# A state-space convolution mixed with a gated feed-forward: rewritten with two equal passes, turned tables and one written order

## The chip, the cores and the metric

The kernel runs on one core of a Trainium2 chip. A core has five instruction streams that run side by side and wait for one another through semaphores: PE (TensorE, matrix products), DVE (VectorE, elementwise), ACT (ScalarE, elementwise with function tables), POOL (GpSimd) and SP (SyncE), which here issues every transfer. Operands lie in SBUF (128 partitions), matrix products land in PSUM (eight banks of 512 float32 values a partition), and inputs, output and spilled intermediates lie in DRAM. The metric is device time in microseconds (us); less is better.

## The reference

The inputs are a sequence of 2048 rows of 640 channels, the parameters of a diagonal state-space model with 128 complex states a channel, and the weights of a gated feed-forward.

```python
g = sigmoid((x * gate_w).sum(-1, keepdims=True))
a = A(x);  b = (gelu(x @ w_gate) * (x @ w_up)) @ w_down       # 640 -> 1728 -> 640
return g * a + (1 - g) * b

def A(u):
    dt = exp(log_dt)[:, None]
    P = exp((dt * (A_re + 1j*A_im))[:, :, None] * arange(L))     # (640, 128, 2048)
    K = einsum("dn,dnl,dn->dl", C, P, dt * B).real               # (640, 2048)
    y = irfft(rfft(pad(u)) * rfft(pad(K)))[:L]                   # a causal convolution of length 2048
    return y + u * Dskip
```

So there are four large pieces of work: the table K from sums of decaying oscillations over 128 states, the convolution of u with K, the two products that widen x to 1728 columns, and the product that narrows them again.

## The kernel before, in words

**K's tables.** A lag is written as l = a + b, with 21 values of a (`A_OF`) and 32 values of b (`b_of`, a multiple of 8). ACT makes the decays exp(a32 * a) and exp(a32 * b) into `eA` and `eB` (`exps`, lines 208 and 211). DVE makes the phases as integers, 65536 to a turn (`trig`, lines 236, 239, 243), ACT their sines and cosines (line 252), and DVE multiplies decays by them (`ktable`, lines 353 to 370). Positive and negative b share a sine up to its sign, so line 367 negates a table. PE contracts over the 128 states (`contract`, lines 382 and 384: 84 columns a product), and `gather` sorts the result with selection matrices (line 405) into `KTt`. This goes by parts of 128 channels, five in all.

**The convolution.** Blocks of 512 rows, c = 0 to 3, are folded (`u_fold`: sum and difference with the rows in reverse, which PE makes with a flip matrix, line 478; the result goes through DRAM as `PMd`), transformed (`u_forward`, line 574), and multiplied with the transformed blocks of K (`k_forward`, line 593, whose evictions are lines 556 and 559) by `products` (lines 631, 635, 636: three planes of K, the third a negated copy made at line 616). `inverse` transforms back (line 647), unfolds and adds u * Dskip (lines 655, 657), and ACT scales with g (line 660). The transform matrices are eleven tables `DFT` (`dft_matrix`).

**The feed-forward.** `ffn_up` makes gate and up for 256 columns of weights at a time (line 428: five products of 512 columns each, into a single bank), ACT or DVE evicts (lines 438 and 440), and SP stores to `GUd` in DRAM (line 441). `down` loads them again, ACT applies gelu (line 694), DVE multiplies (line 695), the result is also spilled to `HTd`, PE contracts over 1728 (line 706), ACT scales by 1 - g (line 708), DVE adds the other half and SP stores the output (`blend`, lines 668 and 669).

**Passes and order.** The second half of the kernel runs in two passes over channels, of 384 and 256 (`PASS`, `DS`): the first makes and spills the gelu product, the second reloads it. The program is written as loops; each engine gets its instructions in an order that a scheduler fixes at build time from the program's order and its own costs, and buffers come from pools that go round. In the first half the list `act` and `some_ups` mix table work with gate/up work; in the second the string of steps F, S, P, I, D, B does it. SP first loads six parameter arrays and u by transposing transfers (lines 133 and 489), then the weights (line 424).

Of the kernel before, what the change touches and what calls it, by code (L numbers as in the profile page):

```python
# [9 lines left out]
ALU = mybir.AluOpType  # L10
# [7 lines left out]
QUARTER = 16384.0  # L18
SIN_SCALE = 2.0 * math.pi / TURN * (1.0 - 2e-7)

A_OF = [0, 1, 2, 3, 4, 5, 6, 7, 256, 258, 260, 262, 512, 516, 768, 772, 1280, 1024, 1536, 1792, 2048]
NA = len(A_OF)
NB_ = 32
NQ = 5


MID = 128
NK = 17  # L30


def b_of(slot):
    return 16 + slot if slot < 16 else 31 - slot
# [3 lines left out]
def kernel(  # L38
# [18 lines left out]
    nc = tc.nc  # L57
    Bsz, L, D = A_u.shape
    N = A_A_re.shape[1]
    F = B_w_gate.shape[1]  # L60
    assert (Bsz, L, D, N) == (1, 2048, 640, 128)
    KT_ = D // 128
    NFT = (F + 127) // 128
    DP = 128
    NP = D // DP
    GP = DP // 4

    PASS = ((0, 1, 2), (3, 4))
    DS = [(DP * p[0], DP * (p[-1] + 1)) for p in PASS]
    DHM = DP * 3  # L70
    DO = D // 2
    NM = 4
# [3 lines left out]

    u_v = u2.rearrange("(c a p e) d -> p c a (e d)", c=4, a=2, p=128, e=2)
    out_v = out2.rearrange("(c a p e) d -> p c a (e d)", c=4, a=2, p=128, e=2)

    last_table = [None]  # L80

    def table(inst):

        if last_table[0] is not None:
            tc.add_manual_dep(inst.ins, last_table[0],
                              mybir.DependencyInfo(mybir.DependencyClass.NoSync, mybir.DependencyReason.DATA),
                              reason="table order")
        last_table[0] = inst.ins.name
        return inst

    def low16(ap):
        return ap.bitcast(I16)

    cp = ctx.enter_context(tc.tile_pool(name="konst", bufs=1))
    dp = ctx.enter_context(tc.tile_pool(name="spill", bufs=1, space=bass.MemoryType.DRAM))
    psC = ctx.enter_context(tc.tile_pool(name="psc", bufs=2, space=bass.MemoryType.PSUM))
    psF = ctx.enter_context(tc.tile_pool(name="psf", bufs=4, space=bass.MemoryType.PSUM))


    NMAT = 11  # L100
    M_E = 10
    DFT = cp.tile([128, NMAT, 2, 512], BF16, name="DFT")
    sel = cp.tile([128, 4, NB_], BF16, name="sel")
    diag = cp.tile([128, KT_, 128], BF16, name="diag")
    ident = cp.tile([128, 128], BF16, name="ident")
    flip = cp.tile([128, 128], BF16, name="flip")
    flipn = cp.tile([128, 128], BF16, name="flipn")
    gwc = cp.tile([128, KT_], BF16, name="gwc")
    KTt = cp.tile([128, NQ, D], BF16, name="KTt")
    T5 = cp.tile([128, D], BF16, name="T5")  # L110
    xT = cp.tile([128, KT_, 2, L // 2], BF16, name="xT")
    g32 = cp.tile([128, 16], FP32, name="g32")
    omg = cp.tile([128, 16], FP32, name="omg")
    rsd = dp.tile([1, 512], FP32, name="rsd")
    HTd = [dp.tile([128, 2, NFT, 256], BF16, name=f"HTd{c}") for c in range(4)]
    PMd = [dp.tile([128, 2, 2, D], BF16, name=f"PMd{c}") for c in range(4)]
    GUd = [[dp.tile([128, NFT, 2, 256], BF16, name=f"GUd{r}_{c}") for c in range(4)] for r in range(2)]

    kctx = ExitStack()
    pp = kctx.enter_context(tc.tile_pool(name="kparams", bufs=1))  # L120
    kb = kctx.enter_context(tc.tile_pool(name="ktab", bufs=1))

    eA = kb.tile([N, 3, NA, DP], BF16, name="eA")
    eB = kb.tile([N, 3, GP, NB_, 4], BF16, name="eB")
    fwk = kctx.enter_context(tc.tile_pool(name="fwork", bufs=2))
    pd = kctx.enter_context(tc.tile_pool(name="dftp", bufs=1))
    kw = kctx.enter_context(tc.tile_pool(name="kwork", bufs=1))
    ictx = ExitStack()
    pw = ictx.enter_context(tc.tile_pool(name="prep", bufs=1))

    def loadT(ap, name):
        t = pw.tile([N, D], BF16, name=name)
        nc.sync.dma_start_transpose(out=t[:], in_=ap[:, :])  # L133
        return t

    ldt = pw.tile([N, D], BF16, name="ldt")
    nc.sync.dma_start(out=ldt[:], in_=A_log_dt.partition_broadcast(N))
    AreT = loadT(A_A_re, "AreT")
    AimT = loadT(A_A_im, "AimT")
    CreT = loadT(A_C_re, "CreT")  # L140
    CimT = loadT(A_C_im, "CimT")
    BreT = loadT(A_B_re, "BreT")
    BimT = loadT(A_B_im, "BimT")
    dskc = pw.tile([128, KT_], BF16, name="dskc")
    nc.sync.dma_start(out=dskc[:], in_=A_Dskip.rearrange("(k p) -> p k", p=128))
    nc.sync.dma_start(out=gwc[:], in_=gate_w.rearrange("(k p) -> p k", p=128))

    xv_i = pw.tile([128, NK], I32, name="xv_i")
    nc.gpsimd.iota(xv_i[:], pattern=[[8, NK]], base=0, channel_multiplier=0)
    xv = pp.tile([128, NK], FP32, name="xv")  # L150
    nc.vector.tensor_copy(out=xv[:], in_=xv_i[:])

# [21 lines left out]
    for q, vals in ((0, (3, 1, 3, 1)), (1, (5, 3, 5, 3))):  # L174
        for g in range(4):
            nc.vector.memset(ncol[32 * g:32 * g + 32, q:q + 1], float(vals[g]))
# [195 lines left out]
    GB = 6  # L372
# [392 lines left out]
```

## Time and profile before

| | |
|---|---|
| time, median of 3 runs | 396.59 us (395.36 to 398.38) |
| span of the profiled execution | 393.3 us; its own time isn't given, 3.3 us lie between this span and the median |
| PE, DVE, ACT busy | 316.4, 302.1, 282.1 us |
| POOL busy | 5.0 us |
| bytes moved by transfers | 68.46 MB |
| granted PE clock, mean | 0.950 |

The span runs from the first to the last instruction. Busy time of an engine is the union of its instructions; a matrix product or an elementwise instruction overlaps the next one by its tail, so two durations in a row add up to more than the time they take. "Idle before" and the list of waits say for how long an engine stood still and what ended that. A window is a stretch of the span, with each engine's busy time in it.

### The profile page before, as it was taken

Reading aid. Unit: us, or ns where it says so; the run is one execution under the profiler, and the core shown is the slowest. Engines: PE = TensorE matmul, PEld = TensorE weight load, DVE = VectorE, ACT = ScalarE, POOL = GpSimd, SP = SyncE. Lnnn points to the kernel's source line nnn. Section 1 sums busy time; section 2 is a strip of 40 time slices with the busy share of each in tenths; the row PEclk is TensorE's granted clock in tenths of the full one; section 3 lists DMA queues with packets and bytes.
Section 4 is the critical chain, followed back from the end, with each engine's and each line's share of the span. In section 5 each row is a group of like instructions: output and inputs, shape, how many; then the busy total and the mean of one; then the engine's idle time right before and its main releaser. Section 6 shows DMA issues by size and latency. Waiting matters only on the chain.

```text
span 393.3 us, 6099 instructions
## 1 busy us (share of the span) xinstructions
PE 316.4 (80%) x2152; PEld 171.5 (44%) x2152; DVE 302.1 (77%) x555; ACT 282.1 (72%) x476; POOL 5.0 (1%) x39
## 2 busy tenths in 40 slices
PE   0019938599999998998379869989998987989994
PEld 0004413235446444544165325535545543557773
DVE  3994999869994989979920399879989798799500
ACT  6955999399986997896866996567669438434333
POOL 5000000000000000000000000000000000000000
PEclk9999987979999999999889977998999998999998
DMA  5893722374664477277449821587980688856760
GB/s 116 155 216 99 213 68 67 105 244 118 184 179 135 133 229 249 85 234 237 163 131 303 230 92 33 128 274 203 286 235 1 182 254 257 270 179 211 226 211 28
DMA packets 96815, 68.46 MB, mean 174 GB/s; under 512 B 22928, under 2 KB 92560, under 8 KB 96784
## 3 DMA queue, kind: packets, MB, share of 16 engines
q1 hardware_dynamic: 96784, 68.07, 60.0%
q8 instruction: 17, 0.28, 0.3%
q14 instruction: 14, 0.11, 0.1%
HBM read 37.96 MB, written 26.48 MB: 164 GB/s over the span
## 4 chain that ended last, share of the span: by engine, by line
PE 50%; ACT 22%; DMA 12%; SPq 6%; DVE 5%; issue 3%; ACTq 0%; DVEq 0%
PE gu L428 17%; PE gu L706 15%; PE cv L593 4%; ACT eA L208 4%; SPq L489 3%; DMA ph<-in_A_u_dram 3%; ACT eB L211 2%; ACT T L252 2%; PE cv L647 2%; ACT HT L694 2%; DMA pm<-PMd 2%; PE cv L405 2%; SPq L133 2%; PE cv L574 2%; PE gu L593 2%
## 5 line engine op out<-in xcount | busy, mean ns | idle before, releaser
L428 PE MATMUL gu<-xT,Wg 128*128 128x512 bf16 (+1 forms) x280 | 73.9, 394 | 39.0 <-DMA Wg<-in_B_w_gate_dram 28.0
L428 PE MATMUL gu<-xT,Wu 128*128 128x512 bf16 (+1 forms) x280 | 73.1, 391 | 2.8 <-ACT GU L438 2.8
L706 PE MATMUL gu<-Wd,HT 128*128 128x384 bf16 (+1 forms) x448 | 70.0, 305 | 3.6 <-DVE HT L695 1.5
L428 PEld LDWEIGHTS <-Wg 128*128 128x128 bf16 (+1 forms) x280 | 27.4, 101 | 74.6 <-DMA Wg<-in_B_w_gate_dram 28.0
L706 PEld LDWEIGHTS <-HT 128*128 128x128 bf16 x448 | 42.4, 99 | 30.7 <-issue 11.4
L438 ACT CAST GU<-gu 128x512 bf16<-128x512 f32 (+1 forms) x78 | 43.9, 603 | 16.6 <-PE gu L428 9.5
L636 DVE TENSOR_TENSOR M<-M,pt 128x1536 bf16<-128x1536 bf16 (+1 forms) x64 | 51.3, 819 | 0.2
L635 DVE TENSOR_TENSOR pt<-Uf,Kf 128x1536 bf16<-128x1536 bf16 (+1 forms) x64 | 50.3, 819 | 0.0
L252 ACT ACTIVATE T<-ph 128x1152 bf16<-128x1152 int16 (+3 forms) x40 | 48.2, 1229 | 1.7 <-DVE ph L243 1.2
L428 PEld LDWEIGHTS <-Wu 128*128 128x128 bf16 (+1 forms) x280 | 28.3, 101 | 37.7 <-issue 7.6
L708 ACT ACTIVATE ob<-gu,omg 128x384 bf16<-128x384 f32 (+1 forms) x32 | 16.7, 524 | 38.7 <-PE gu L706 38.7
L694 ACT ACTIVATE HT<-HT 128x3328 bf16<-128x3328 bf16 (+1 forms) x16 | 27.1, 1692 | 9.5 <-DMA HT<-GUd 9.5
L668 DVE TENSOR_TENSOR ob<-ob,zt 128x768 bf16<-128x768 bf16 (+1 forms) x16 | 7.8, 492 | 30.2 <-ACT ob L708 19.6
L440 DVE CAST GU<-gu 128x512 bf16<-128x512 f32 x34 | 22.5, 685 | 7.8 <-PE gu L428 7.7
L631 DVE TENSOR_TENSOR M<-Uf,Kf 128x1536 bf16<-128x1536 bf16 (+1 forms) x16 | 12.9, 818 | 18.0 <-ACT Kf L559 17.4
L574 PE MATMUL cv<-pm,DFT 128*128 128x256 bf16 (+1 forms) x112 | 20.5, 319 | 6.4 <-ACT Uf L556 3.8
L593 PEld LDWEIGHTS <-DFT 128*128 128x128 bf16 (+1 forms) x160 | 14.9, 100 | 24.5 <-issue 19.1
L211 ACT ACTIVATE eB<-a 128x384 bf16<-128x384 f32 (+1 forms) x64 | 23.2, 453 | 0.9 <-DVE a L198 0.9
L593 PE MATMUL cv<-KTt,DFT 128*128 128x256 bf16 (+2 forms) x96 | 21.1, 319 | 2.8 <-ACT Kf L556 1.9
L236 DVE SCALAR_TENSOR_TENSOR ph<-b,phi 128x128 int32<-128x128 f32 x105 | 22.4, 296 | 0.0
L647 PE MATMUL cv<-M,DFT 128*128 128x384 bf16 (+1 forms) x128 | 21.3, 314 | 0.9 <-ACT pr L651 0.5
L556 ACT ACTIVATE Kf<-cv 128x512 bf16<-128x512 f32 (+1 forms) x24 | 15.5, 668 | 8.0 <-PE cv L593 8.0
(121 smaller groups left out, 449.1 us busy)
## 6 DMA issues: line engine op xcount, KB each, us to landing
GUd<-GU SPq DMA_DIRECT2D x104, 128.0 KB, 2.6
HT<-GUd SPq DMA_DIRECT2D x8, 832.0 KB, 6.1
Ut<-GUd SPq DMA_DIRECT2D x8, 832.0 KB, 7.6
HTd<-HT SPq DMA_DIRECT2D x8, 832.0 KB, 4.1
HT<-HTd SPq DMA_DIRECT2D x8, 832.0 KB, 4.8
Wg<-in_B_w_gate_dram SPq DMA_DIRECT2D x12, 320.0 KB, 3.6
Wu<-in_B_w_up_dram SPq DMA_DIRECT2D x12, 320.0 KB, 4.2
ph<-in_A_u_dram SPq DMA_DIRECT2D x4, 640.0 KB, 4.1
```

Of the source, the lines that this page charges most:

```text
L211: table(nc.scalar.activation(out=eB[:, s0:s0 + np_, :, sl, :], in_=src.rearrange("n (p g d) -> n p g d", p=np_, d=4), func=ACT.Exp, scale= ...
L252: table(nc.scalar.activation(out=dst, in_=phl, func=ACT.Sin, scale=SIN_SCALE))
L428: nc.tensor.matmul(p[:fsz].rearrange("p (a e q) -> p a e q", a=2, e=2), lhsT=wt[key][:, kt, f0:f0 + fsz], rhs=xT[:, kt, :, 256 * c:256 * ( ...
L438: nc.scalar.copy(out=t[:fsz], in_=p[:fsz])
L440: nc.vector.tensor_copy(out=t[:fsz], in_=p[:fsz])
L574: nc.tensor.matmul(pU[ri][:, 0:W], lhsT=dmat(e, ri, m), rhs=pm[:, ri, e, 0:W], start=(e == 0), stop=(e == 1))
L593: nc.tensor.matmul(pW[ri][:, 0:W], lhsT=lhs, rhs=rhs, start=(first and x == 0), stop=(x == len(seq) - 1), skip_group_check=not first)
L635: tt(out=tv, in0=ux, in1=kx, op=ALU.mult)
L636: tt(out=Mv, in0=Mv, in1=tv, op=ALU.add)
L647: nc.tensor.matmul(pY[:, r, 0:W], lhsT=dinv(m, r, e), rhs=M[m // 2][:, r, m % 2, 0:W], start=(m == 0), stop=(m == NM - 1))
L694: table(nc.scalar.activation(out=HT[:p1, fs], in_=HT[:p1, fs], func=ACT.Gelu_apprx_tanh))
L706: nc.tensor.matmul(pD[:, 0:W], lhsT=HT[:fsz, ft, 128 * e:128 * e + 128], rhs=Wd[:fsz, ft, 0:W], start=(ft == 0), stop=(ft == NFT - 1))
```

## The change

The kernel is written anew; the inputs, the output and the method (tables, contraction, block transforms, gated feed-forward) stay.

- *Two equal passes.* Both passes take 320 channels (`W = 320`), for K's tables, the spectra, the products and the way back. Gate and up are evicted two banks (1024 columns) at a time (steps G, GE, GS), in two halves of the sequence, p = 0 and 1. The down step D contracts for both passes at once, into the two banks of one pair, so nothing is spilled to `HTd`.
- *Tables turned by 45 degrees.* Both phases get an eighth of a turn more (`EIGHTH`). With both tables at 45 degrees the two terms of a cosine of a sum get the same sign, and b and -b use the same two sines with their places changed, so there is no negation.
- *Shared transform matrix.* Forward and inverse transforms of u use one matrix `DM`; K has five matrices `KM`, with windows already in them, and the last lags come in as one small product (`sel` by `RR`) in step Y. K's spectrum has two planes; DVE subtracts where it added the negated plane.
- *Transfers.* Parameters are loaded straight and turned by PE (`TA`, `TB`, `TC`), and so is the first half of u (`TX`); the second half still comes by ten transposing transfers (`LT`). The reversed rows come by a transfer in DRAM (`rev`, `URd`). K is sorted by transfers through DRAM (`KD`, `KL`, `KZ`, `KR`) instead of selection matrices.
- *Written order and places.* `ORDER` names 814 steps; each engine runs its share of them in this order, with no scheduler. `MEM` gives each buffer its place in one SBUF tile (`arena`), and four pairs of PSUM banks are taken in turn. `ON_DVE` names the evictions that DVE does; ACT does the rest.

What the letters of the steps mean: phB, phA phases, snB, snA sines, tmB, tmA table products, xB, xA decays (digits: pass, chunk); KC contraction, KE its eviction; U forward transform, UE eviction; W0 to W3 spectra of K, S0 to S3 evictions; P products (pass, output block c, input block i); Q inverse, QE eviction, Y unfold, Z or X scaling by g; LH, LV loads of gate and up, HG gelu, HM product, D down, O or B scaling by 1 - g; OS output store. Of each output tile one of Z and O writes and one of B and X adds to it, in the order in which they come.

The diff, cut to its core:

```diff
-    PASS = ((0, 1, 2), (3, 4))
-    DS = [(DP * p[0], DP * (p[-1] + 1)) for p in PASS]
+W = 320
+ORDER = """
+ident Lx00 Lx01 Lw030 Lw000 Lw001 LAim Lldt LAre Lx10 Lx11 LCre Lw031 Lw040 LCim LBre LBim iota TX00 TX02 fill EX00 cols
...
+tmB10 KD00 GS118 KD01 G111 GE19 phB12 GS19 G119 Lw131 GE111 GS111 tmB11 snB12 G125 Lw100 GE119 Lw151 phB13 GE125 GS119 GS125
...
+KC10 FO1 KE15 KC12 KE10 KC14 GG FO2 KE12 KC13 KE14 FO0 KC16 KE13 KC11 KE16 U022 KE11 U021 UE022 KD11 U013 KD10 KD13 KD12
+UE021 U002 UE013 U010 UE002 U001 FO3 UE010 U000 U003 UE000 UE001 U032 UE003 U031 UE032 P000 U012 UE031 KR13 KL1 KR12 U011
...
+LV10 D010 O1001 LH10 Y101 O1010 B0001 B0010 OS0001 D011 P122 OS0010 HG100 Q110 LH11 B0011 X1010 OS0011 O1011 Q111 HM100
...
+"""
+        for j in range(4):
+            @step(f"phB{h}{j}")
+            def _(h=h, j=j, dsl=dsl):
+                p = w(f"phB{h}{j}")
+                for x in range(4):
+                    DVE.tensor_scalar(out=p[:, 0, x], in0=r("b32")[:, dsl], scalar1=float(8 * (4 * j + x + 1)), scalar2=EIGHTH,
+                                      op0=ALU.mult, op1=ALU.add)
+                DVE.tensor_scalar(out=p[:, 1], in0=low16(p[:, 0])[:, :, ::2], scalar1=-1.0, scalar2=QUARTER, op0=ALU.mult,
+                                  op1=ALU.add)
...
+                tt(out=X[:, :, pos], in0=T[1][:, :, 0:4 * n], in1=E[:, :, pos], op=ALU.mult)
+                tt(out=X[:, :, neg], in0=T[0], in1=E[:, :, neg], op=ALU.mult)
+                tt(out=E[:, :, pos], in0=T[0][:, :, 0:4 * n], in1=E[:, :, pos], op=ALU.mult)
+                tt(out=E[:, :, neg], in0=T[1], in1=E[:, :, neg], op=ALU.mult)
...
+                @step(f"P{h}{c}{i}")
...
+                    if j == 0:
+                        tt(out=M[:], in0=u[0], in1=K[:], op=ALU.mult)
+                    else:
+                        a = w(f"t{h}{c}{i}a")
+                        tt(out=a[:], in0=u[0], in1=K[:], op=ALU.mult)
+                    tt(out=b[:], in0=u[1], in1=K[:], op=ALU.mult)
+                    if j % 2 == 0:
+                        if j:
+                            tt(out=M[:], in0=M[:], in1=a[:], op=ALU.add)
+                        tt(out=M[:, 0], in0=M[:, 0], in1=b[:, 1], op=ALU.subtract)
+                        tt(out=M[:, 1], in0=M[:, 1], in1=b[:, 0], op=ALU.add)
+                    else:
+                        tt(out=M[:, 1], in0=M[:, 1], in1=a[:, 0], op=ALU.add)
+                        tt(out=M[:, 0], in0=M[:, 0], in1=a[:, 1], op=ALU.subtract)
+                        tt(out=M[:], in0=M[:], in1=b[:], op=ALU.subtract)
...
+                @step(f"D{c}{e}{a}")
+                def _(c=c, e=e, a=a):
+                    p = take(f"PD{c}{e}{a}", 2)
+                    H, Wd = r(f"H{c}{e}", ["m0", "m1"]), r("Wd", ["z", None])
+                    for f in range(NFT):
+                        for h in range(2):
+                            PE.matmul(p[:, h, 0:W], lhsT=H[:, f, 128 * a:128 * a + 128], rhs=Wd[:, f, W * h:W * h + W],
+                                      start=(f == 0), stop=(f == NFT - 1))
...
+                    @step(f"B{h}{c}{e}{a}")
...
+                        DVE.scalar_tensor_tensor(out=z[:], in0=r(f"PD{c}{e}{a}")[:, h, 0:W], scalar=r("gg", 1)[:, 2, t:t + 1], in1=z[:],
+                                                 op0=ALU.mult, op1=ALU.add)
+                        give(f"PD{c}{e}{a}")
...
+    with tc.manual_schedule():
+        for name in ORDER.split():
+            run(steps, name)
```

More of the change, by code (lines that the diff above doesn't have):

```diff
@@ L6 @@
 from concourse import mybir
-from concourse.masks import make_identity
 from concourse._compat import with_exitstack
@@ L57 @@
     nc = tc.nc
+    PE, DVE, ACTE, POOL, SP = engines(nc)
     Bsz, L, D = A_u.shape
@@ L74, with step, put @@
+    pp = ctx.enter_context(tc.tile_pool(name="psum", bufs=1, space=bass.MemoryType.PSUM))
+    arena = cp.tile([128, ARENA // 2], BF16, name="arena")
+    pairs = [pp.tile([128, 2, 512], FP32, name=f"ps{i}") for i in range(4)]
+    mem = Memory(arena, pairs, MEM)
+    add, r, w, take, give = mem.add, mem.r, mem.w, mem.take, mem.give
+    steps = {}
+    def step(name):
+        def put(fn):
+            steps[name] = fn
+            return fn
+        return put
     u2 = A_u.rearrange("b l d -> (b l) d")
@@ L114 @@
[L114 to L123, printed above, removed]
@@ L711 @@
[L711 to L736 removed]
+    URd = dp.tile([4, 256, D], BF16, name="URd")
```

1441 lines of the change are left out of this document (856 added, 585 removed).

## The prediction

> **What bounds the kernel now.** I read the page's busy times, then a table of windows, then the list of waits.
>
> ```profile
> PE 316.4 (80%) x2152; PEld 171.5 (44%) x2152; DVE 302.1 (77%) x555; ACT 282.1 (72%) x476; POOL 5.0 (1%) x39
> ```
>
> Windows (us; busy PE, PEld, DVE, ACT, POOL, granted clock, DMA share, GB/s), then waits (in total, times, longest us):
>
> ```profile
> 0.00:28.00 28.00, 0.00 (x0) 0.00 (x0) 20.15 (x59) 21.81 (x40) 4.98 (x39) 1.00 0.85 156
> 28.00:200.00 172.00, 148.17 (x953) 71.53 (x954) 147.30 (x313) 142.14 (x245) 0.00 (x0) 0.94 0.53 160
> 200.00:220.00 20.00, 17.97 (x244) 11.26 (x241) 1.59 (x2) 15.35 (x35) 0.00 (x0) 1.00 0.90 256
> 220.00:360.00 140.00, 122.97 (x731) 68.22 (x731) 122.32 (x164) 89.80 (x129) 0.00 (x0) 0.94 0.62 185
> 360.00:393.30 33.30, 27.26 (x232) 20.45 (x230) 10.71 (x20) 12.96 (x29) 0.00 (x0) 0.97 0.55 168
> ```
> ```profile
> PE gu L428 <- DMA Wg<-in_B_w_gate_dram: 28.0, 1, 28.0
> ...
> DVE M L631 <- ACT Kf L559: 17.4, 1, 17.4
> ```
>
> No engine is full; the bound changes by stage. Until 28 us PE has nothing, for its first weights stand behind 16 transposing DMAs on SP's queue. From 28 to 200 DVE, PE and ACT share the K tables and the gate/up products, DVE 147.30/172 = 86% busy. At 200 to 220 DVE stands still (1.59 busy) until the first spectra exist. From 220 to 360 DVE and PE are both 87% busy, and the last 33 us belong to PE's down products. DVE idles 393.3 - 302.1 = 91 us, in the 200 window and the last alone 18 + 23.
>
> **Prices.** A busy time counts each instruction's tail, which overlaps the next one; so I price by start to start, in runs without a wait.
>
> ```profile
> 227.65 0.95 DVE L631 TENSOR_TENSOR M<-Uf,Kf 128x1536 bf16<-128x1536 bf16 x1
> 228.52 0.95 DVE L636 TENSOR_TENSOR M<-M,pt 128x1536 bf16<-128x1536 bf16 x1
> ...
> 308.36 0.69 DVE L636 TENSOR_TENSOR M<-M,pt 128x1024 bf16<-128x1024 bf16 x1
> 308.96 0.69 DVE L635 TENSOR_TENSOR pt<-Uf,Kf 128x1024 bf16<-128x1024 bf16 x1
> ...
> 360.76 1.28 DVE L635 TENSOR_TENSOR pt<-Uf,Kf 128x1024 bf16<-128x1024 bf16 x2
> 361.96 1.41 DVE L636 TENSOR_TENSOR M<-M,pt 128x1024 bf16<-128x1024 bf16 x2
> ...
> 41.85 1.88 DVE L440 CAST GU<-gu 128x512 bf16<-128x512 f32 x3
> ...
> 50.45 2.31 DVE L236 SCALAR_TENSOR_TENSOR ph<-b,phi 128x128 int32<-128x128 f32 x11
> ...
> 59.09 0.89 DVE L301 TENSOR_SCALAR ph<-fr,tcol 128x256 int32<-128x256 f32 x3
> ...
> 5.74 13.32 ACT L211 ACTIVATE eB<-a 128x384 bf16<-128x384 f32 x32 [0.90 <-DVE a L198]
> ...
> 103.08 1.24 PE L428 MATMUL gu<-xT,Wg 128*128 128x512 bf16 x5
> 104.16 1.24 PE L428 MATMUL gu<-xT,Wu 128*128 128x512 bf16 x5
> ...
> 308.90 4.88 PE gu L706 x28
> ...
> 374.04 3.54 PE gu L706 x28
> ```
>
> DVE on bf16: 0.87 us at 1536 columns, 0.60 at 1024, so 0.52 ns a column + 0.07 us. A pair whose second reads what the first wrote lasts 1.41 in place of 1.28: 0.12 us for each such neighbour. From PSUM or on f32: (1.88 - 0.68)/2 = 0.60 at 512 and 2.31/11 = 0.2 at 128, so 1.04 ns a column + 0.07. The table's f32 scaling: 0.26 at 256, some 0.29 at 320. ACT: 13.32/32 = 0.416 at 384, 0.83 ns a column + 0.10 us. PE: 1.08/5 = 0.216 at 512; (4.88 - 0.33)/27 = 0.169 at 384, (3.54 - 0.27)/27 = 0.121 at 256, so 0.14 at 320.
>
> **The change, part by part.** Everything is rewritten, so I sum each engine over the 814 steps.
>
> PE: 54 gate/up steps x 10 x 0.216 = 117; down 448 x 0.137 = 61; U and Q 256 x 0.137 = 35; 112 spectrum matmuls (160 before) 15; Y 16; K contraction 12; turning of inputs, gate 7. Sum 263 at full clock, 280 at the 0.94 that before was granted; less than any sum that follows for DVE.
>
> DVE: products P, 52 of 2560 columns at 1.40 and 40 of 1280 at 0.735, 102; K tables phA, phB, tmA, tmB 24.5 + 15.2 + 23.0 + 23.7 = 86; 37 copies out of PSUM (17 GE at 1.13 among them) 34; 32 final multiply-adds at 0.42, 13; HM 16 at 1.0, 16; folds 7; preparation 30. Sum 288. Some 75 instructions read what their neighbour has just written: 75 x 0.12 = 9. **DVE 297**, about what it is now. The turn by 45 degrees saves L367's negations and the two planes those of L616, but 17 gate/up copies of double width stay on DVE.
>
> No row shows bf16 at 2560 columns or in runs of 16. From below I take nothing off; from above stands the f32 rate, 1.04, which would add 0.52 x (52 x 2560 + 40 x 1280) = 96 us. I take 0.52, since 1024 and 1536 with the same broadcast run at it.
>
> ACT: 226 of work, 282 now; 51 exponentials in place of 106 (they span both passes), no fold or gather copies. Against that stand 13 table loads where there are 8.
>
> ```profile
> 42.93 0.72 ACT L278 ACTIVATE vi<-vi 128x640 f32<-128x640 f32 x1
> 43.67 1.28 ACT L208 ACT_TABLE_LOAD   x1
> 44.96 8.78 ACT L208 ACTIVATE eA<-a 128x384 bf16<-128x384 f32 x21
> ...
> 1.55 3.35 POOL L160 IOTA c_i<- 32x1 int32 x20
> ```
>
> A load costs 1.28: the activation before ends at 43.65, the one behind starts at 44.96.
>
> [...]
>
> SP: the 16 transposes of the start become 10 later ones, HTd and PMd vanish (16 x 832 KB among them), so DMA, 0.62 busy at most over a long window, falls. SP stays one queue: GS and weights behind LT wait some 10 x 1.3 = 13 us, at a time when PE has slack.
>
> **The path.** (a) *Front, ACT.* POOL's 20 small iotas end near 7 us; DVE's column steps and `fr` near 9.7; from there ACT runs sines, tables, dt and copies to 29 (18.4 by the prices). Then up to snB00 and at: 51 exponentials x 0.63 = 32.3, sq, rr, rw 9.4 with their four loads, four GE 3.7, the sine load 1.3, snB00 2.3, at 0.6: 50; phi and ACT's own waits 2. The first table product tmB00 starts at **81**. DVE has done 51 of its 297 by then and waited 30. PE needs 49 of these 81 us and is covered.
> (b) *DVE from tmB00 to its last product P130:* 297 - 51 - 4 (the last sums) = **242**. ACT's time at the same steps is its work + 12, DVE's its work + 30: ACT is ahead. The 20 us of standstill go, since pass 1's tables fill DVE while KD and KL carry pass 0's K through DRAM.
> (c) *Stalls.* Nothing in before shows this order. Bounds: 0 below; above, before's own looseness (108/0.856 - 108 = 18 in the table stage, 133/0.874 - 133 = 19 among the products). I take **15**: 6 (tmA14 on its sine, KE on KC, P000 on the last U after seven KC) and 9 among the products, where PE has 114 us at full clock, 121 at 0.94, beside DVE's 133.
> (d) *Tail* behind P130: Q130 and Q131 2.3, QE 0.7, Y131 1.1, X 1.0, and the store, from its issue to the span's end 393.3 - 389.6 = 3.7: **9**.
>
> ```profile
> 389.58 1.25 SPq L669 DMA_DIRECT2D out_dram<-ob  x2
> ```
>
> 81 + 242 + 15 + 9 = 347 us of span. Around before's span lie 396.6 - 393.3 = 3.3 us, the median of its runs (395.4 to 398.4) standing for the profiled execution's own time, which the page doesn't give. **350 us**, 12% below before. A change of 1% is what a measurement of this kernel can just tell, by the spread of those runs.
>
> **New waits.** Every down step D takes one of four PSUM pairs and gives it back only when DVE's B0 and ACT's O1 have read both halves; before, ACT alone emptied it. B0 stands behind a product P of 4.3 or 5.8 us on DVE, and behind B0 stand HM and the next P; PE's next steps wait for the pair. With four pairs and a D of 3.9 us one such wait is covered, two in a row aren't. The loads LH and LV write where an earlier D has read (H00, H10 and H20 share a place): LH10 can start when D001 ends and takes some 6 us, HG and HM 2 x (1.6 + 1.0), while D010, D011 and Y101 give PE 9; the 2 us left are in the nine.
>
> ```profile
> HT<-GUd SPq DMA_DIRECT2D x8, 832.0 KB, 6.1
> ```
>
> **Rivals.**
> 1. *As loose as now.* The order is no better than before's: stalls 18 + 19 in place of 15, so 350 + 22 = **372**. For it: two engines beside one another were 87% busy each from 220 to 360, and PE's clock fell there to 0.94. Against: PE's need among the products is smaller (114 for 133 of DVE), and DVE's standstill at 200 has a cause that is gone.
> 2. *Tighter.* All stalls covered, iotas hidden: 350 - 15 - 3 = **332**. For it: ACT leads DVE by 18 us after tmB00, room that the sum doesn't use.
> [...]
> 4. *Slower: the pairs stand behind P.* If B0 of most D's waits out a whole P while PE holds nothing else that it can start, each costs about 5 us. 350 + 16 x 5 = 430 if all sixteen are bare; from ten on (46/5) the kernel is slower than before; with twelve it is **410**. For it: DVE takes its work in the written order, and P is the longest instruction chain there is. Against: Q, Y, U and the other pairs lie between.
> 5. *Work without gain.* DVE's sum is 297 beside 302. If it idled 91 us as it does now, 297 + 91 + 3 = **391**: within 1.5% of before. Against: 18 of the 91 lie in a window whose cause is removed, and the last stage no longer runs on PE alone.
> 6. *Slow shapes.* With the f32 rate on the 2560 columns, **446**.
>
> **How the numbers follow.** Forecast, 335 to 365: 0.60. Rival 1 (365 to 385): 0.16. Rival 2 (below 335): 0.11. Rival 3: 0.02, inside the forecast's own range. Rival 4: 0.05. Rival 5: 0.04. Rival 6: 0.02. The range 332 to 374 takes the forecast, rival 3, half of rival 2 and two thirds of rival 1: 0.60 + 0.02 + 0.06 + 0.11, about 0.8. Faster by over 1%: 0.60 + 0.16 + 0.11 + 0.02 and a quarter of rival 5, 0.90; within 1% 0.03; slower 0.07.
>
> **What the changed profile would show.** (a) right: PE's first gate/up matmul before 20 us, tmB00 (lines 684 to 687) first at 78 to 85, ACT busy 90% between 10 and 80; wrong: ACT waiting for PE or for stores there. (b) right: DVE busy near 300 in all, 2560 columns at 1.40 from start to start, no window of 20 us after tmB00 under 80%; wrong: a standstill before the first P. (c) right: DVE waits for PE and ACT of some 15 us in total behind tmB00; rival 4 would be seen as DVE's line 1130 and PE's line 1121 at the head of the waits. (d) right: 9 us from the last P to the end. What would upset the sum most is a front in which stores, ten transposes and weights on the one queue keep the gate/up steps back, so that ACT, which takes their evictions in order, stands still.

## The result: slower, and the profile after

The changed kernel takes **462.25 us** (median of 4 runs, 459.79 to 464.41), beside 395.98 us for the kernel before (390.72 to 398.38): a ratio of **1.176** (95% interval 1.160 to 1.192). The forecast was 350 us, the range ended at 374. The profiled execution's span is 462.6 us where the sum said 347, so 115.6 us are to be found. Of the four runs of e13 below, one (390.33 us, at a granted clock of 0.897 where the others have 0.902 to 0.918) belongs to a slower state of the chip and is left out.

The page of the changed kernel, busy time of each engine, then its two costliest eviction rows (busy, mean ns of one), by line and shape:

```profile
PE 311.9 (67%) x2002; PEld 179.2 (39%) x2002; DVE 308.4 (67%) x449; ACT 274.0 (59%) x280; POOL 10.5 (2%) x46
...
L839 ACT CAST arena<-ps 128x1008 bf16<-128x1008 f32 x9 | 38.8, 4651 | 1.8 <-PE ps L731 1.8
L843 DVE CAST arena<-ps 128x1008 bf16<-128x1008 f32 x3 | 13.3, 4438 | 2.3 <-PE ps L731 2.3
```

DVE's sum is near its forecast (297). ACT was to have 226 of work and has 274; nine instructions of one form take 38.8 of that, 4.65 us each. They are K's evictions, step KE, which I had priced like any other copy, at some 0.9 us.

Busy time by windows of 20 us (PE, PEld, DVE, ACT, POOL, clock, DMA share, GB/s) shows where the engines stand still:

```profile
40.00:60.00 20.00, 11.30 (x114) 6.01 (x113) 5.46 (x15) 19.87 (x32) 0.00 (x0) 0.78 0.64 127
...
100.00:120.00 20.00, 10.95 (x50) 4.79 (x49) 4.07 (x7) 6.35 (x7) 0.00 (x0) 0.90 0.42 139
...
180.00:200.00 20.00, 3.80 (x18) 1.64 (x17) 3.20 (x5) 2.51 (x3) 0.00 (x0) 0.69 0.60 180
...
260.00:280.00 20.00, 7.65 (x44) 4.57 (x44) 3.78 (x3) 15.47 (x4) 0.00 (x0) 0.50 0.12 22
...
360.00:380.00 20.00, 14.60 (x111) 10.27 (x109) 9.45 (x11) 1.98 (x4) 0.00 (x0) 1.00 0.52 145
```

At 180 to 200 no engine is a fifth busy, at 100 to 120 only PE is over half; at 260 to 280 ACT is busy on four instructions, and PE and DVE mostly stand. The list of waits (in total, times, longest us) says what ended them:

```profile
ACT arena L1106 <- DMA arena<-GUd: 24.7, 5, 8.9
ACT arena L839 <- DMA KDd<-arena: 23.3, 2, 18.5
...
DVE arena L843 <- DMA GUd<-arena: 17.9, 2, 13.7
DVE arena L696 <- DMA GUd<-arena: 17.6, 2, 16.4
DVE arena L1112 <- DMA arena<-GUd: 14.8, 4, 6.1
...
DVE arena L684 <- DMA KDd<-arena: 14.4, 1, 14.4
DVE arena L843 <- DMA KDd<-arena: 11.1, 1, 11.1
...
PE ps L1121 <- DVE arena L1130: 5.7, 2, 5.1
```

All but the last of these rows end with a transfer: stores to `GUd` (gate/up), stores to `KDd` (K), and loads of H and V from `GUd`. Yet DMA is only 0.38 busy behind the first table product (last row below). And the waits for `KDd` are odd: line 684 is a table product, the wait of 18.5 us at line 839 is that of a gate/up eviction, and the 11.1 at line 843 are those of another eviction, at 280.3 us; none of them touches a byte of K.

DVE from the first table product (91.8 us) to the end of the last P (451.2 us):

```profile
91.77 0.81 DVE L684 TENSOR_TENSOR arena<-arena 128x1280 bf16<-128x1280 bf16 x1
...
449.71 1.49 DVE L1027 TENSOR_TENSOR arena<-arena 128x2560 bf16<-128x2560 bf16 x1
```
```profile
91.80:451.20 359.40, 245.17 (x1619) 145.84 (x1618) 253.03 (x314) 194.79 (x182) 0.63 (x1) 0.84 0.38 111
```

So against the sum: front 91.8 for 81 (+10.8); behind it 359.4 for 257 (+102.4), of which 253 is work (forecast 242; the slow form of K's four evictions on DVE is the difference, as e1 shows) and **106 is standstill (forecast 15)**; tail 462.6 - 451.2 = 11.4 for 9 (+2.4). By DVE's list of waits in that window 73 of the 106 us end with a transfer (stores to `GUd` 18, stores to `KDd` 30, loads of H and V 15, output stores 10), the rest with PE or ACT.

### The profile page after: what moved, and what is told of

The parts are those of the page before. It is cut to its first block, busy times and chain, and to the rows that moved or that the text cites. A ratio compares the mean times of both kernels' runs of the same rounds, so it can differ in the third digit from the quotient of the medians.

```text
span 462.6 us, 5343 instructions
## 1 busy us (share of the span) xinstructions
PE 311.9 (67%) x2002; PEld 179.2 (39%) x2002; DVE 308.4 (67%) x449; ACT 274.0 (59%) x280; POOL 10.5 (2%) x46
## 5 line engine op out<-in xcount | busy, mean ns | idle before, releaser
L873 PE MATMUL ps<-arena 128*128 128x512 bf16 x540 | 135.8, 413 | 57.8 <-ACT arena L839 35.6
L839 ACT CAST arena<-ps 128x640 bf16<-128x640 f32 (+3 forms) x91 | 106.0, 1252 | 74.1 <-DMA KDd<-arena 23.3
L873 PEld LDWEIGHTS <-arena 128*128 128x128 bf16 x540 | 55.9, 104 | 134.7 <-issue 63.8
L1121 PE MATMUL ps<-arena 128*128 128x320 bf16 x448 | 68.8, 317 | 12.3 <-DVE arena L1112 6.4
L843 DVE CAST arena<-ps 128x1024 bf16<-128x1024 f32 (+4 forms) x27 | 40.7, 1535 | 43.7 <-DMA GUd<-arena 17.9
L1121 PEld LDWEIGHTS <-arena 128*128 128x128 bf16 x448 | 45.9, 103 | 34.0 <-DVE arena L1112 11.7
L1106 ACT ACTIVATE arena<-arena 128x1792 bf16<-128x1792 bf16 x16 | 26.5, 1694 | 24.7 <-DMA arena<-GUd 24.7
L702 ACT ACTIVATE arena<-arena 128x2560 bf16<-128x2560 int16 (+1 forms) x10 | 24.4, 2444 | 16.0 <-DVE arena L718 9.4
L940 PE MATMUL ps<-arena 128*128 128x320 bf16 x128 | 24.4, 352 | 11.5 <-ACT arena L839 8.1
L1018 DVE TENSOR_TENSOR arena<-arena 128x2560 bf16<-128x2560 bf16 x20 | 29.7, 1486 | 2.7 <-DMA out_dram<-arena 2.7
L1038 PE MATMUL ps<-arena 128*128 128x320 bf16 x128 | 22.4, 331 | 11.6 <-ACT arena L841 8.5
L950 PE MATMUL ps<-arena 128*128 128x320 bf16 x112 | 20.3, 325 | 11.8 <-ACT arena L841 5.4
L1112 DVE TENSOR_TENSOR arena<-arena 128x1792 bf16<-128x1792 bf16 x16 | 17.0, 1088 | 16.6 <-DMA arena<-GUd 14.8
L730 PE MATMUL ps<-arena 128*128 128x84 bf16 x160 | 15.4, 217 | 15.9 <-ACT arena L839 11.4
L669 ACT ACTIVATE arena<-arena 128x1280 bf16<-128x1280 int16 x16 | 19.8, 1282 | 6.7 <-DVE arena L687 3.0
L940 PEld LDWEIGHTS <-arena 128*128 128x128 bf16 x128 | 14.3, 113 | 20.4 <-issue 13.0
L1051 PE MATMUL ps<-arena 128*128 128x320 bf16 x64 | 15.3, 329 | 9.0 <-ACT arena L839 9.0
L650 ACT ACTIVATE arena<-arena 128x640 bf16<-128x640 f32 x31 | 20.7, 729 | 0.2
L1038 PEld LDWEIGHTS <-arena 128*128 128x128 bf16 x128 | 13.6, 106 | 18.6 <-issue 11.9
L841 ACT ACTIVATE arena<-ps 128x640 bf16<-128x640 f32 x29 | 18.5, 718 | 3.6 <-DMA GUd<-arena 1.6
```

Of the source, the lines that this page charges most:

```text
L650: ACTE.activation(out=o, in_=r("a32")[:].rearrange("p (h g w) -> p h g w", h=2, w=4), func=ACT.Exp, scale=float(8 * b), **kw)
L702: ACTE.activation(out=w(f"TA{h}{j}")[:], in_=low16(r(f"phA{h}{j}")[:])[:, :, :, ::2], func=ACT.Sin, scale=SIN_SCALE)
L839: ACTE.copy(out=o, in_=src)
L841: ACTE.activation(out=o, in_=src, func=ACT.Copy, scale=scale)
L843: DVE.tensor_copy(out=o, in_=src)
L873: PE.matmul(t[:, c, :].rearrange("p (e q) -> p e q", e=2), lhsT=lhs, rhs=xt[:, kt, :, 256 * cc:256 * cc + 256], start=(kt == 0), stop=(kt ...
```

## The experiments

Four suspects follow from the rows above: the form of K's evictions; the one queue, with its transposes and the reversal of u; what ties `KDd` to unrelated steps; and the places of H and V. The first kernels change one thing each; later ones start from the best before them. Line numbers move by one to six between kernels, in e4 by 34. The kernel before ran beside each group of experiments; its medians, 394.49, 394.82, 395.63 and 394.91 us, differ by 1.1 us, so a difference of that size between groups says nothing.

### e1: K evictions in runs; e4: four forms side by side

```diff
-                o = w(f"Kraw{h}", i)[:].rearrange("p a w g -> p g (a w)")
+                o = w(f"Kraw{h}", i)[:].rearrange("p a w g -> p (a w) g")
...
-copy_on(f"KE{h}{i}", o[:, g0:g0 + 12].rearrange("p (b g) x -> p b g x", b=2), p[:, :, 0:504].rearrange("p b (g x) -> p b g x", g=6))
+copy_on(f"KE{h}{i}", o[:, :, g0:g0 + 12].rearrange("p x (b g) -> p x b g", b=2), p[:, :, 0:504].rearrange("p b (g x) -> p x b g", g=6))
```

> The changed kernel, with the K evictions walking the destination in runs of 12 (or 6) neighbouring elements, and PSUM with a step of 84, instead of PSUM in a row and the destination in single elements 160 bytes apart. Theory 1 (the scattered write is what makes a K eviction cost 4.65 us on ACT and 4.44 us on DVE, and it stands on the path in both passes): an eviction falls to 0.9 to 1.4 us, the busy time of the 14 groups from 57 to 13-18 us, and the kernel from 462 to 415-430 us. Rival (the price is PSUM's side or the size of the copy): an eviction stays over 3 us and the kernel within 8 us of 462. Rival (evictions cost that much, but other waits end last behind them): evictions fall as in theory 1, and the kernel only to 445-455.

Measured: **435.71 us**, ratio to before 1.108 (1.101 to 1.115). Rows of e1 by line and shape:

```profile
L839 ACT CAST arena<-ps 128x1008 bf16<-128x1008 f32 x9 | 8.5, 998 | 2.3 <-PE ps L731 2.3
L843 DVE CAST arena<-ps 128x1008 bf16<-128x1008 f32 x3 | 3.6, 1205 | 1.5 <-PE ps L731 1.5
```

The same copy of the same numbers to the same places takes 1.0 us in place of 4.65 on ACT, 1.2 in place of 4.44 on DVE. All fourteen groups go from some 57 us to 13, of which the kernel gets 26.5. That is 5.7 us less than theory 1 gave at least: the evictions were on the path in both passes, but not for all of their time. In pass 0 DVE's first table product behind them comes 7.4 us earlier (186.23 for 193.67), still after a wait for `KDd`; the rest was gained in pass 1.

> The changed kernel, with four forms of the K eviction side by side (K comes out in another order; every other step is the changed kernel's). In pass 0: flat write and flat read (groups 0, 2 on ACT, 3 on DVE), flat write and read with a step of 84 elements (1, 6 on ACT, 4, 5 on DVE). In pass 1: single elements 160 bytes apart and flat read (0, 2, 4 on ACT), runs of 12 elements and read with a step of 84 (1, 3, 5 on ACT, 6 on DVE). Theory 1: only the form with single elements stays at 4.6 us, the three others take 0.9 to 1.4 us. Rival (reads from PSUM with a step are as dear as scattered writes): the second and the fourth form take over 3 us, and e1 gains nothing. Rival (any copy of 1008 columns in three dimensions is slow): all but the flat one over 3 us.

e4, whose K comes out in another order, took 443.73 us in one run. Its timeline, of DVE and then ACT in pass 0 (start, duration, count):

```profile
159.44 1.20 DVE L877 CAST arena<-ps 128x1008 bf16<-128x1008 f32 x1
161.98 1.21 DVE L877 CAST arena<-ps 128x1008 bf16<-128x1008 f32 x1 [1.34 <-PE ps L733]
```
```profile
160.18 1.90 ACT L873 CAST arena<-ps 128x1008 bf16<-128x1008 f32 x2 [0.75 <-PE ps L733]
...
166.72 0.98 ACT L873 CAST arena<-ps 128x1008 bf16<-128x1008 f32 x1
```

Both reads cost the same: in a row (DVE 159.44, ACT's two at 160.18, 0.95 each) or with a step of 84 floats (161.98, 166.72). Only the write counts, and only when single 2-byte elements lie 160 bytes apart (4651 ns on ACT and 4438 on DVE in the changed kernel); runs of 12 elements are as good as a flat row (e1: 998 ns on ACT, 1205 on DVE). With the step of 160 bytes that is 4.4 ns a column on DVE and 4.6 on ACT, in runs 1.2 and 1.0.

### e2 and e6: the reversal of u; e3: the transposes

SP's queue in the changed kernel (start us, us in issue), then what the DMA engines moved from 104 to 115 us, in 40 slices (busy tenths, GB/s):

```profile
39.20 14.80 SPq L831 DMA_TRANSPOSE arena<-in_A_u_dram  x10
...
104.54 0.62 SPq L785 DMA_DIRECT2D URd<-in_A_u_dram  x1
105.27 8.91 SPq L886 DMA_DIRECT2D GUd<-arena  x1
```
```profile
DMA  2011010520122222222222222222222222222225
GB/s 79 33 33 42 14 51 9 33 9 9 47 84 102 98 98 98 102 98 98 102 98 98 102 98 93 107 93 98 102 98 98 102 98 98 98 102 98 98 102 217
```

The reversal moves 1280 KB, while it runs alone at a steady 98 to 102 GB/s with the engines 2 tenths busy; at that rate it takes 13 us (an estimate). From 107 to 113 us the DMA share is 0.27 at 99 GB/s; as a mean over 16 engines it doesn't tell whether four of them are full or all a quarter busy. The store behind the reversal takes 8.91 us only to be issued and 15.9 to land, where the median of its form is 2.5.

```diff
-GE08 LXR3 LXR0 LXR1 LXR2 rev phA00                                (e2: rev moved)
+Lw011 Ldsk Lgw rev LT00 LT01 ...
-LT00 LT01 LT02 LT03 LT04 LT10 LT11 xA15 LT12 LT13 GE00 LT14        (e3: spread)
+GS06 LT01 ... GS013 LT00 ... GS07 LT02 ... GS017 LT14 ... GE018 GL
-            SP.dma_start(out=URd[:], in_=src)                      (e6, on e1)
+            POOL.dma_start(out=URd[:], in_=src)
```

> The changed kernel, with one step moved: the reversal of u from DRAM to DRAM is issued ahead of the ten transposes (at about 39 us) instead of at 104.5 us. Theory 2 (that transfer, 1.25 MB on about a quarter of the DMA engines for 13 us, holds the gate/up store behind it, 15.9 us to landing, so buffers come free late, and DVE and ACT stand still from 105 to 121 us): the standstill of DVE at 105-121 goes to under 5 us, and the kernel from 462 to 446-454 us. Rival (the time is only moved: transposes and weights at 39-60 us become later by as much, and the first tmB step starts at 95 us or later instead of 91.8): the kernel within 4 us of 462.

Measured: 460.88 us, ratio 1.173 (1.163 to 1.183): **the rival**. DVE's first table product:

```profile
102.44 0.81 DVE L683 TENSOR_TENSOR arena<-arena 128x1280 bf16<-128x1280 bf16 x1
```

The standstill at 105 to 121 is gone, and the front is 10.7 us longer. The hold costs what it costs wherever a wanted transfer stands behind it.

> The changed kernel, with the ten transposes of u spread, one behind each of ten gate/up stores, instead of in one row of 14.8 us on SP at 39.2 us, and the step GL, which reads them all, behind the last. Theory 3 (the row of transposes holds stores and weight loads back, so buffers come free late, and DVE stands 13.7 us at 43-57 us for them): the first tmB step starts at 80-85 instead of 91.8 us, and the kernel falls to 450-456 us. Rival (that stretch is bound by ACT's exponentials, and DVE's idle time there is cover): first tmB within 2 us of 91.8, kernel within 4 us of 462.

Measured: 459.79 us, ratio 1.171 (1.163 to 1.179). The first table product comes at 87.5 instead of 91.8, so theory 3 has a part of the front, 4.3 of the 10.8 us, though not the 80 to 85 that it gave. Of these the kernel gets 2.5, within its spread and within the rival's 4: the standstill behind (16.5 us) stays and starts earlier.

> e1 with the reversal of u issued on GpSimd's queue instead of SP's, at the same place of the order. Theory (the standstill at 105-121 us comes from the gate/up stores that queue behind this transfer in the same queue): DVE's wait of 16.5 us there falls under 6 us, and the kernel from 435.7 to 420-427 us. Rival (the transfer holds the DMA engines themselves, whichever queue it came by): the wait stays at 12 us or more, kernel within 5 us of 435.7.

Measured: 433.48 us, ratio 1.100 (1.092 to 1.107), 2.2 us below e1. The named wait (16.5 at 121 us) shrinks to two of 2, and a new one of 12.1 ends at 106.7:

```profile
DVE arena L662 <- DMA GUd<-arena: 12.1, 1, 12.1
...
DVE arena L696 <- DMA GUd<-arena: 4.2, 2, 2.1
```

GpSimd issues the transfer at 85.9 instead of 104.5, having nothing else to do, and the stores, now in another queue, are still late: six that SP issues from 88.74 to 99.36 us take 5.42 and 5.10 us in issue, where in the changed kernel the same four and two take 2.54 and 1.69. For the time the rival holds. What the stores wait for isn't shown; another queue did not free them.

### e5 and e7: down weights, output stores; e8: all of it

```diff
-Lxa0 Lxa3 phB11 LWd G19              (e5, on e1)
+W303 S303 GS12 LWd W302
-                        SP.dma_start(out=out_v[c, a, :, ee, W * h:W * h + W], ...      (e7, on e1)
+                        POOL.dma_start(out=out_v[c, a, :, ee, W * h:W * h + W], ...
```

> e1 with one step moved: the load of the down weights (2080 KB) is issued behind the last gate/up stores of pass 0 (about 225 us) instead of at 170 us. In e1 it is followed on the one queue by weights and the stores of K, DVE waits 16.5 us for the first store of K (to 186 us) and ACT 22.6 us. Theory (the load of the down weights makes that standstill): DVE's wait there falls under 5 us, and the kernel from 435.7 to 418-426 us. Rival (the stores of K are late because the evictions behind them are late: PE waits for a gate weight, which is queued anyway): standstill stays over 10 us, kernel within 5 us of 435.7.

Measured: 430.21 us, ratio 1.089 (1.082 to 1.097): 5.5 us, between both expectations. DVE's wait for `KDd` falls from 16.5 to 8.9 us and not away; something else holds it.

> e1 with the 32 stores of the output issued on GpSimd's queue instead of SP's. Theory (in the last stage, loads of H and V stand on SP behind stores that wait for DVE's last sums, so ACT waits 25.3 us and DVE 15.4 us for loads of H and V): these waits fall by half or more, and the kernel from 435.7 to 415-425 us. Rival (the loads are late because their buffers are still held by products): waits stay within 8 us in sum, kernel within 5 us of 435.7.

Measured: 436.94 us, ratio 1.109 (1.100 to 1.117): nothing. ACT's and DVE's waits for loads of H and V fall from 40.7 to 30.4 us in sum, but ACT then waits 10.7 us for DVE at the same line. The rival holds for the time: the loads are late for another reason.

> e1 with all of it: transposes spread as in e3, reversal of u and the stores of the output on GpSimd's queue, down weights moved as in e5. Theory (the time above the forecast is the K evictions and the one queue): gains of e3, e5, e6 and e7 add up, 435.7 to 375-395 us. Rival (each standstill that goes uncovers the next wait of the written order): 405-425 us.

Measured: 424.32 us, ratio 1.075 (1.068 to 1.082): the four gains, 2.5 + 5.5 + 2.2 - 1.2 = 9, add up (11.4), but they are small: the rival holds, and the queue's order was not the main thing.

### e9 and e10: the false dependence

What is odd in the list of waits can be read in the program as it is built, where each instruction has its semaphores (the changed kernel first, e9 below):

```
111 L752 DMACopy KDd0_69<-arena_63 32x21x80 [waits DMAHW2_49,DMAHW3_49,DMAHW1_49,DMAHW4_49,DMAHW0_49,DMAHW5_49,DVE_49,DMAHW6_49,Activation_49,Pool_49]
111 L754 DMACopy KDd0_71<-arena168064_64 32x21x80 [waits DMAHW1_49,DVE_49,Activation_49]
```

`KD` reads every fourth partition, `k[x::4, :, x, :]`, of a buffer that is a part of the one block `arena`. In the changed kernel the first store of K waits for seven of the eight DMA semaphores, with the down weights behind one of them, and the next writer in the block on each engine waits for the stores of K, whatever it writes. In the same program none of the 60 gate/up stores, which read the block without such a step, waits for more than one DMA semaphore. So the framework that sets the semaphores takes the step in the partitions for the whole block. That the step is what widens the dependence is read from the built program; e9 tests that it goes by the block.

```diff
-    arena = cp.tile([128, ARENA // 2], BF16, name="arena")
+    arena = [cp.tile([128, (hi - lo) // 2], BF16, name=f"arena{lo}") for lo, hi in zip(CUTS, CUTS[1:])]
+CUTS = (0, 168064, 198784, ARENA)
```

> e1 with the one block of memory made of three (cut at 168064 and 198784 bytes, every buffer where it was), and nothing else. In the program as built, the first store of K (L752, which reads every fourth partition of Kraw) waits for seven of the eight DMA semaphores, and steps that touch no byte of Kraw (tmB10, phB12, the next gate/up evictions) wait for the four stores of K: their reads with a step in the partitions are taken for reads of the whole block. With three blocks these waits are gone from the built program. Theory 4 (this false dependence is what holds DVE 16.5 us and ACT 22.6 us at 165-190 us, and some 5 us again in pass 1): the standstill shrinks to under 6 us, the kernel falls from 435.7 to 412-424 us. Rival (the waits are there, but PE's gate weight or the down weights end last at the same place): ACT's wait there stays over 12 us, kernel within 5 us of 435.7.

Measured: **416.30 us**, ratio 1.055 (1.042 to 1.068), 19.4 us below e1: theory 4. All waits of DVE and ACT for `KDd`, 53.7 us together in e1, are gone from e9's list; the longest standstill of ACT from 160 to 200 us, expected under 6, is now this one, behind a gate/up store:

```profile
188.24 1.27 ACT L671 ACTIVATE arena<-arena 128x1280 bf16<-128x1280 int16 x1 [6.55 <-DMA GUd<-arena]
```

> e8 with the block of memory made of three, as in e9. Theory 4: from 424.3 to 402-414 us; ACT's wait of 15.8 us at 165-181 us falls under 5 us. Rival: within 5 us of 424.3.

Measured: 405.71 us, ratio 1.030 (1.020 to 1.040), 18.6 below e8: the same gain on another ground. ACT's longest wait from 165 to 181 us is now 4.46. How much of e5's gain is the same microseconds wasn't separated.

### e11: places of H and V

In e8 the chain that ended last holds these pieces behind 300 us (start, us):

```profile
307.45 5.32 DMA arena<-GUd
...
319.46 6.46 DMA arena<-GUd
...
355.02 5.33 DMA arena<-GUd
...
368.31 6.57 DMA arena<-GUd
...
387.17 5.71 DMA arena<-GUd
```

That is 29 us of loads on the path. SP's own list of waits from 290 to 400 us shows what they stand for, products above all:

```profile
SPq L1099 <- DVE arena L1027: 24.0, 2, 14.5
```

Each load writes where a product or an earlier H or V lay, so it can't start before that is read, although from P031 and P032 on two places of over 7 KB a partition, and one from FO0 on, are not used again.

```diff
-V00:140032 V10:137472 V31:127232 V01:137472 V11:127232 H21:79360 H01:102656 H20:120064
+V00:198784 V10:198784 V31:198784 V01:188544 V11:188544 H21:188544 H01:157824 H20:157824
-P030 LV00 ... Z0311 LV01 ... P110 LV10 ... Y100 LV11 ... P120 LV31 ... D310 LH21
+QE001 LV00 ... P032 LV01 ... HM000 LV10 ... HM010 LV11 ... HM101 LV31 ... HM110 LH21
```

> e10 with eight of the buffers of H and V at places that are free earlier, and nine of their sixteen loads issued ahead by 4 to 70 steps of the order. In e8 five such loads of 5.3 to 6.6 us each stand in the chain that ends last, because a load can only start when the buffer that shares its place is read. Theory 5 (written places of H and V put load latencies on the path in the last stage): at least four of the five leave the chain, waits of ACT and DVE for loads of H and V fall from 22 us to under 8, the kernel is 12 to 25 us faster than e10. Rival (PE's down products or the P products set that stage, and the loads are late only as much as they may be): within 5 us of e10.

Measured: **389.42 us** (10 runs), ratio 0.987 (0.983 to 0.991), 16.3 us below e10: theory 5, and the first that is faster than the kernel before. Waits of ACT and DVE for loads of H and V, in e8 22.5 us, are one row, 9.3 where under 8 was expected:

```profile
ACT arena L1108 <- DMA arena<-GUd: 9.3, 4, 5.8
```

and behind 300 us the chain has no load any more. e11 moves places and issue together, since a load that is issued earlier to an occupied place waits there (24.0 us in SP's list above); what each is worth alone was not run.

### e12, e13, e14: the reversal in four, a pair given back

```diff
-    src = bass.AP(u2.tensor, u2.offset + 255 * D, [[512 * D, 4], [-D, 256], [1, D]])                  (e12)
+    src = bass.AP(u2.tensor, u2.offset + (255 - 64 * x) * D, [[512 * D, 4], [-D, 64], [1, D]])         # rev0 to rev3
+GS010 rev0 ... GS120 rev1 ... GS17 rev2 ... GS126 rev3
-    ACTE.copy(out=b[:, 0], in_=r("PL")[:, 0, 0:16]); give("PL")            # in GT, pass 1            (e13)
+    ACTE.copy(out=w("gb", 0)[:, 0], in_=r("PL")[:, 0, 0:16]); give("PL")   # step GC, behind GL
```

> e11 with the reversal of u in four transfers of 320 KB, spread behind four gate/up stores between 110 and 150 us on SP's queue, instead of one of 1280 KB. In e11 it runs at about 99 GB/s on about a quarter of the DMA engines from 91 to 105 us, stores behind it land late, and ACT stands 14.1 us, DVE 8.0 us. Theory 2b (what costs is the length of the hold on those engines while stores are waited for): no wait of ACT or DVE over 6 us between 85 and 125 us, and the kernel from 389.4 to 376-384 us. Rival (the same hold in four pieces is paid four times in smaller waits, or the next wait ends last): within 4 us of 389.4.

Measured: 384.04 us, ratio 0.970 (0.964 to 0.976), 5.4 below e11. No wait over 6 us is left between 85 and 125 us; the longest are 5.61 (ACT for DVE) and, on DVE, 3.19:

```profile
111.45 1.01 ACT L842 CAST arena<-ps 128x1024 bf16<-128x1024 f32 x1 [5.61 <-DVE arena L688]
```

Theory 2b, with the gain at the foot of what it gave: some of the hold is paid in smaller waits.

> e11 with the pair of PSUM banks of step GL given back right behind GL by a copy of its 16 columns, instead of in pass 1 with the tanh of GT, so that four pairs go round instead of three for some 110 us. Theory 6 (PE's waits for evictions, 34.9 us in ten, are a shortage of pairs): the kernel from 389.4 to 380-386 us. Rival (PE waits there because evictions wait for their destination, whatever the pairs): within 3 us of 389.4.

Measured: 384.89 us (384.50 to 388.77), ratio 0.976 (0.969 to 0.983). The median lies in theory 6's range, 4.5 below e11, but the interval overlaps e11's (0.983 to 0.991), and one of the three runs lies within the rival's 3 us. Inconclusive by itself.

> e11 with the edits of e12 and e13 together. Theories 2b and 6: 370-380 us. If both rivals hold: within 4 us of 389.4.

Measured: **380.64 us** (379.91 to 382.21), ratio 0.963 (0.958 to 0.969): 3.7% faster than the kernel before, with the changed kernel's arithmetic, and 0.6 above the range expected. The two edits together give 8.8 us, alone 5.4 and 4.5. From e12 to e14 PE's gate/up products wait 13.4 us for ACT's evictions instead of 20.8, but 10.9 for their weights instead of 5.0, so theory 6 has at most part of it. The page, DVE from its first table product to its last P, and its longest waits in that window:

```profile
PE 290.9 (77%) x2002; PEld 171.5 (45%) x2002; DVE 296.1 (78%) x449; ACT 240.6 (64%) x280; POOL 27.8 (7%) x78
```
```profile
89.50:368.40 278.90, 226.73 (x1611) 139.14 (x1610) 240.48 (x314) 161.88 (x181) 13.12 (x24) 0.91 0.48 140
```
```profile
DVE arena L698 <- ACT arena L704: 6.8, 4, 2.5
DVE arena L846 <- PE ps L733: 6.5, 3, 4.5
DVE arena L1020 <- DMA out_dram<-arena: 5.0, 1, 5.0
```

DVE's standstill there is 38 us, in the changed kernel 106. By the list 20 of the 38 end with ACT, 8 with PE, 6.5 with output stores and 4 with gate/up stores; none ends with a load of H or V.

## Why the prediction was wrong, step by step

**DVE's sum, right.** 297 was forecast; e14, where K's evictions have their normal form, has 296.1, of which 240.5 lie between the first table product and the last P (forecast 242). Products at 2560 columns run at 1.40 us from start to start (289.74, 291.14), so the slow-shapes rival was out. Tables in runs of 16 lose nothing either: 1280 columns, priced at 0.735, take 0.73 us from start to start (changed kernel, 92.49 to 93.22). Rows of the changed kernel, on DVE and ACT:

```profile
289.74 1.49 DVE L1014 TENSOR_TENSOR arena<-arena 128x2560 bf16<-128x2560 bf16 x1
291.14 1.48 DVE L1018 TENSOR_TENSOR arena<-arena 128x2560 bf16<-128x2560 bf16 x1
...
329.34 1.28 ACT L1106 ACT_TABLE_LOAD   x1
330.64 1.70 ACT L1106 ACTIVATE arena<-arena 128x1792 bf16<-128x1792 bf16 x1
```

Rival 3, with its 0.02, took a switch of tables to cost more than its load, and no run shows such a term: a load takes 1.28 us and the activation starts within 0.02 of its end (329.34 and 330.64 above), also in the front (e14: loads at 69.88 and 71.93, activations at 71.17 and 73.22).

**Work of ACT, and the "37 copies out of PSUM" of DVE, wrong in K's evictions.** I priced K's evictions by their columns and didn't look at how they write. The rows gave no such write, so the step should have had bounds like the other unknown shapes. They cost 44 us of busy time and 26.5 of the kernel (e1). ACT in e14 still has 240.6 us where 226 was forecast; those 15 were not taken apart. PE's sum used 0.137 us for a product of 320 columns where the line through its own two prices gives 0.145; in e14 one is 3.98/28 = 0.142, and nothing hangs on it.

**(a) Front, wrong by 10.8 us.** The first gate/up product is in time (19.48 us). The term "GS and weights behind LT wait some 13 us, at a time when PE has slack" was read as free: spreading the transposes brings 4.3 back (e3). What I named as the thing that would upset the sum, one queue in the front, did happen, but it is a small part. In e14 ACT is 64.5 of 70 us busy between 10 and 80, and the first table product still comes at 89.5. From 29.6 us to the end of `at` (84.6) ACT's work is 50.3 us, as priced (50), so the sum of work holds; what it had too small are the waits, 2 us for `phi` and all of ACT's own. ACT waits 4.7 us on the way, and 4.9 more pass from `at` to the first table product. There ACT waits 2.0 us for PE ahead of GC, the copy that e13 put in, and makes the sine snB01 (line 671) only then; and DVE's step `phi` waits for that sine:

```profile
88.86 0.73 DVE L632 TENSOR_SCALAR arena<-arena 128x640 f32<-128x640 f32 x1 [2.52 <-ACT arena L671]
```

`MEM` gives `phi` and `phB01`, which the sine reads, the same place (143744): a written place again. In e12, which has no GC, `phi` starts at 86.66 after a wait of 0.34, so the copy costs 2.2 us of the front.

**(b) "The 20 us of standstill go, since pass 1's tables fill DVE while KD and KL carry pass 0's K", wrong.** KD itself stopped DVE: its false dependence made it a barrier for later writers on every engine (19.4 us, e9). The change list said that K goes through DRAM; that a read with a step in the partitions orders against the whole block can't be seen in the diff or in the old trace, but it stands in the built program's waits, which I hadn't read for that. In pass 1 K's slow evictions filled the same place (260 to 280 us).

**(c) Stalls, wrong: 15 forecast, 106 found, 38 left in e14.** This is the step that failed most. The 15 were waits of DVE for ACT and PE; of the 106 some 73 end with a transfer, which the sum held at nothing but for 2 us. The bounds came from the looseness of the old order, which a scheduler with its own pools had made; they say nothing of an order with written places. The paragraph on new waits had LH and LV right in kind (a load can only start where an earlier D has read, and takes some 6 us) and then put 2 us on one of them, where five stood on the path (16.3 us, e11). The reversal wasn't in the sum at all, as a transfer of 1280 KB with DMA 0.62 busy seemed to fit anywhere; the store behind it lands 15.9 us after its issue, and as one piece on GpSimd's queue it costs 5.4 us more than as four spread on SP's (e12).

**(d) Tail:** 11.4 for 9, in e14 10.1.

**Rivals.** "Pairs stand behind P" was the case on the right side, by the wrong mechanism: line 1121 waits for line 1130 5.7 us in two waits. The time lay outside the range because several things that I held at nothing or at a normal price came in a row, each on the path. From the changed kernel to e14 the steps are 26.5 (K's evictions, e1), 11.4 (the queue, e8), 18.6 (the false dependence, e10), 16.3 (places of H and V, e11), 5.4 (the reversal, e12) and 3.4 (the pair, e14; by its interval not apart from zero), in all 81.6. The other 30.6 us to the forecast lie in e14's front (89.5 for 81), behind it (278.9 for 257) and in its tail (10.1 for 9). Behind the front the work is as forecast and the stalls are 38 for 15: waits of DVE for ACT and PE come to 28, waits for stores to 11. Which of them a better order or other places would remove was not tested.

## What to carry to other kernels

Price a copy by how it writes as well as by its columns (4.65 and 1.0 us for the same 1008 here), and give a form that no row shows an upper bound. Where buffers have written places and one order, read the built program's semaphores for waits between steps that share no byte, and ask of each load in a late stage when its place falls free, not when its queue does. A standstill that ends with a transfer isn't a full DMA (DMA was 0.38 busy behind the first table product): moving transfers about in the order and among queues gave 11 us here, removing what made them wait (e10, e11) gave 35.

## What the runs showed of the hardware

Writing single 2-byte elements 160 bytes apart costs 4.65 us for 1008 columns on ACT and 4.44 on DVE, against 1.0 and 1.2 for runs of 12 (e1); reading PSUM with a step of 336 bytes took 0.98 us on ACT and 1.21 on DVE, in a row 0.95 and 1.20 (e4). The reversal, 1280 KB from DRAM to DRAM, moved 98 to 102 GB/s at a DMA share of 0.27, and issuing it from another engine's queue didn't free the stores behind it (e6: a wait of 12.1 us). Ten transposing transfers took 14.8 us in issue on SP, about what I had allowed (13). PE's granted clock was 0.50 at 260 to 280 us of the changed kernel, where PE had 7.65 us of work.
